# Decay products by two scans on 96 partitions, and another order of loads and first units, in a chunked attention with a gated feed-forward network

## The chip, the cores and the metric

One core of one Trainium2 chip. The time is device time of one execution in microseconds (us), the median of several runs. Each run also has a profile's span, which is about 2 us shorter than its time. Ratios of two kernels are the mean time of the one's fast runs over the mean time of the other's fast runs of the same rounds on the same chip, so they are not quite the ratio of the medians quoted; the interval behind a ratio is its 95% interval. A run is called slow when it is over 1.5% above the fastest run of the same kernel. "Granted clock" is the TensorE clock that the throttle allowed, as a share of full speed; row PEclk of a page gives it in tenths.

## The reference

A linear attention with decay (4 batches, 8 heads, 768 tokens, state 16, head size 32), whose output, put together as 3072 tokens of 256, goes through a gated network with 1536 hidden columns.

```python
log_a = np.log(np.clip(a, 1e-06, 1.0))
for c in range(nc):                         # chunks of the sequence
    cum = np.cumsum(la, axis=-1)
    L = np.exp(cum[:, :, :, None] - cum[:, :, None, :]) * causal
    M = np.einsum('bhin,bhjn->bhij', Cc, Bc) * L
    y_intra = np.einsum('bhij,bhjd->bhid', M, xc)
    y_inter = np.einsum('bhin,bhnd->bhid', Cc, state) * np.exp(cum)[:, :, :, None]
    y[:, :, sl] = y_intra + y_inter
    state = decay_full * state + sum_j(Bx)
# then: ((y2 @ w_a) * (y2 @ w_b)) @ w_out
```

## The kernel before

The sequence is cut into six blocks of 128 tokens. Two batches of one block are a pair, so there are twelve pairs; pair 0 is the first two batches' block 0. For each pair the kernel loads B, C and x (`bn`, `cn`, `xn`), scales B and C with factors of the running product of `a`, transposes them, forms scores, masks them and multiplies by x: this last is the value product. The result feeds units (pair, part), each 8 matmuls with `Wa` and `Wb`. Units are what TensorE is filled with while other engines prepare the next pair.

The head issues its transfers from three engines. SyncE's queue begins with `a`, then come the first halves of B, C and x; ScalarE's queue carries the second halves; GpSimd issues the weights.

```python
    nc.sync.dma_start(a_sb, a.rearrange("b h (k q) -> (b h) k q", q=Q))   # 32 rows
    load1(nc.scalar, 0, 0, 1)      # B of pair 0
    load1(nc.sync, 0, 0, 0)
    load1(nc.scalar, 0, 1, 1)      # C of pair 0
    load1(nc.sync, 0, 1, 0)
    ...
    nc.gpsimd.memset(sel, 1.0)     # masks, then the identity, then the weights
    ...
    load_w(0)                      # first third of Wa, Wb
    ...                            # causal mask
    load_w(1, (0,))                # second third, Wa only
```

The decay products are six scans on 32 partitions (row = batch and head), one for each block, spread over the head. Factors for block 0 come first; those of blocks 1 to 5 follow as 40 small matmuls between units (0,1) and (0,2). Then:

```python
    go((0, 4))                     # a unit between the masks of pair 1 and its value product
    pv(1)                          # value product of pair 1
    state(0)
    state(1)
    go((0, 5), (1, 0), (1, 1), (1, 2))
    transposes(2)
```

## Time and profile before

| | before |
|---|---|
| time, median of 4 (lowest to highest) | 130.28 us (129.74 to 130.97) |
| span of the profiled run | 128.0 us |
| TensorE busy | 93% |
| (0,0), first unit, begins | 10.82 us |
| transposes of pair 1 / of pair 2 begin | 14.52 / 24.86 us |
| first output product begins | 28.18 us |

The prediction below shows the lines that carry this. The profile lines of the head that matter later were not among them; here is the timeline of all engines of the kernel before (start, length, engine and line, operation; in brackets the idle time before and what ended it):

```profile
0.79 0.40 SPq L132 DMA_DIRECT2D a_sb<-in_a_dram  x1
...
2.28 0.94 POOL L188 DMA_DIRECT2D Wa<-in_moe_w_a_dram  x1
...
5.43 0.41 DVE L262 TENSOR_TENSOR cm<-cn,fC 128x256 f16<-128x256 f32 x1
...
7.03 1.25 PE L201 MATMUL tc<-warm 128*128 128x512 f16 x5
...
8.72 0.63 ACT L247 ACTIVATE x<-xn 128x512 f16<-128x512 f32 x1 [0.94 <-DMA xn<-in_x_dram]
```

The load of `a` costs SyncE 0.40 us of issuing, GpSimd issues the first weights at 2.28, C of pair 0 is used at 5.43 without a wait, and x of pair 0 is in at 8.72. Warm-up matmuls work on nothing and are there to keep TensorE busy.

### The profile page before, as it was taken

How to read it: one execution, taken by the hardware profiler on the slowest of the kernel's cores; microseconds unless marked ns; L12 is line 12 of the kernel's file. 1: busy time of each engine (PE TensorE's matmuls, PEld its weight loads, DVE VectorE, ACT ScalarE, POOL GpSimd, SP SyncE). 2: the span in 40 equal slices, each digit the busy share in tenths (PEclk: the TensorE clock that was granted, in tenths of full speed). 3: DMA queues.
4: the chain of work that ended last, by engine and by line, in shares of the span. 5: the costliest groups of instructions: out<-in, count | busy, mean ns of one | idle time of the engine just before them, and what ended most of it. 6: DMA issues, size and time to landing. Idle time of an engine off the chain costs nothing.

```text
span 128.0 us, 4399 instructions
## 1 busy us (share of the span) xinstructions
PE 118.6 (93%) x1761; PEld 97.1 (76%) x1761; DVE 89.6 (70%) x178; ACT 66.5 (52%) x129; POOL 62.0 (48%) x106
## 2 busy tenths in 40 slices
PE   6969979799999999999999999999999999999960
PEld 2425757688887888888888888888888888888840
DVE  4676769658695976967958959959759569364420
ACT  3344567594836545455556456465445464564410
POOL 7966830799982925907828447338339100000000
PEclk9999999999999999999999999999999999999999
DMA  3999999775435666566456555565565310211203
GB/s 66 158 215 164 211 199 216 117 136 111 105 67 88 156 90 111 120 110 142 91 96 146 104 87 131 111 111 123 101 133 116 73 42 0 46 41 23 51 8 82
DMA packets 51555, 13.76 MB, mean 107 GB/s; under 512 B 45328, under 2 KB 51504, under 8 KB 51536
## 3 DMA queue, kind: packets, MB, share of 16 engines
q1 hardware_dynamic: 46560, 10.72, 43.8%
q0 software_dynamic: 3184, 2.36, 12.5%
q10 hardware_dynamic: 1792, 0.41, 1.6%
q8 instruction: 13, 0.21, 0.7%
q14 instruction: 6, 0.05, 0.1%
HBM read 11.13 MB, written 3.15 MB: 111 GB/s over the span
## 4 chain that ended last, share of the span: by engine, by line
PE 77%; DMA 9%; SPq 7%; POOL 1%; issue 1%; ACTq 1%; DVE 0%; POOLq 0%
PE ops L493 25%; PE aps L476 22%; PE bps L476 21%; DMA cn<-in_C_dram 9%; SPq L123 7%; PE SC L380 3%; PE SC L336 3%; PE SC L397 2%; ACTq L123 1%; POOL bm L262 1%; PE SC L313 0%; POOL cm L262 0%; DVE osb L506 0%; POOLq L451 0%; POOLq L262 0%
## 5 line engine op out<-in xcount | busy, mean ns | idle before, releaser
L486 DVE TENSOR_TENSOR hk<-bps,asb 128x512 f16<-128x512 f32 x72 | 49.2, 687 | 20.8 <-ACT asb L485 18.9
L485 ACT COPY asb<-aps 128x512 f32<-128x512 f32 x72 | 42.1, 587 | 17.9 <-PE aps L476 16.4
L476 PE MATMUL bps<-X2T,Wb 128*128 128x256 f16 x288 | 43.2, 273 | 1.1 <-ACT G L611 1.1
L476 PE MATMUL aps<-X2T,Wa 128*128 128x256 f16 x288 | 43.5, 273 | 0.1
L493 PE MATMUL ops<-Wo,hk 128*128 128x256 f16 x288 | 35.3, 273 | 0.0
L476 PEld LDWEIGHTS <-Wb 128*128 128x128 f16 x288 | 28.1, 98 | 4.5 <-issue 0.6
L493 PEld LDWEIGHTS <-hk 128*128 128x128 f16 x288 | 27.4, 98 | 4.1
L476 PEld LDWEIGHTS <-Wa 128*128 128x128 f16 x288 | 26.8, 98 | 4.8 <-issue 0.3
L370 DVE TENSOR_TENSOR t<-SC,causal 128x512 f16<-128x512 f32 x45 | 29.4, 681 | 1.3 <-ACT tmp L367 1.0
L451 POOL TENSOR_TENSOR sbd<-U,maskbd 128x512 f16<-128x512 f32 x10 | 11.5, 1154 | 21.1 <-DVE U L447 21.0
L508 ACT ACTIVATE osb<-ops 128x256 f32<-128x256 f32 x23 | 8.8, 383 | 23.6 <-PE ops L493 22.9
L249 POOL TENSOR_SCALAR x<-xn 128x512 f16<-128x512 f32 x9 | 13.4, 1489 | 0.8 <-DMA xn<-in_x_dram 0.2
L408 ACT ACTIVATE X2T<-SC 128x512 f16<-128x512 f32 x11 | 6.6, 597 | 5.1 <-PE SC L380 5.1
L262 POOL TENSOR_TENSOR bc<-cn,fC 128x128 f16<-128x128 f32 x16 | 6.1, 402 | 5.6 <-DMA cn<-in_C_dram 3.4
L262 POOL TENSOR_TENSOR t<-bn,fB 128x256 f16<-128x256 f32 x12 | 7.7, 639 | 0.1
L262 POOL TENSOR_TENSOR bc<-bn,fB 128x128 f16<-128x128 f32 x16 | 6.1, 401 | 0.0
L380 PEld LDWEIGHTS <-x 64*32 64x32 f16 x384 | 3.2, 91 | 3.2 <-ACT x L247 1.6
L201 PE MATMUL SC<-warm 128*128 128x512 f16 (+1 forms) x14 | 4.4, 453 | 1.2 <-DVE warm L150 1.2
L427 DVE STREAM_TRANSPOSE dt<-SC 128x64 f32<-128x64 f32 x9 | 2.2, 249 | 4.1 <-ACT X2T L408 4.1
L262 POOL TENSOR_TENSOR cm<-cn,fC 128x128 f16<-128x128 f32 (+1 forms) x5 | 2.1, 445 | 5.9 <-DMA cn<-in_C_dram 5.9
L368 POOL TENSOR_TENSOR t<-tmp,causal 128x512 f16<-128x512 f32 x3 | 3.5, 1156 | 3.1 <-ACT tmp L367 3.1
L380 PE MATMUL SC<-t,x 64*32 64x144 f16 (+1 forms) x352 | 4.8, 224 | 0.0
(69 smaller groups left out, 66.8 us busy)
## 6 DMA issues: line engine op xcount, KB each, us to landing
xn<-in_x_dram SPq DMA_DIRECT2D x23, 128.0 KB, 3.2
out_dram<-osb SPq DMA_DIRECT2D x46, 64.0 KB, 2.1
bn<-in_B_dram SPq DMA_DIRECT2D x23, 64.0 KB, 2.7
cn<-in_C_dram SPq DMA_DIRECT2D x23, 64.0 KB, 3.3
Wa<-in_moe_w_a_dram POOLq DMA_DIRECT2D x3, 256.0 KB, 6.8
Wb<-in_moe_w_b_dram POOLq DMA_DIRECT2D x3, 256.0 KB, 6.6
Wo<-in_moe_w_out_dram POOLq DMA_DIRECT2D x1, 768.0 KB, 10.2
xn<-in_x_dram ACTq DMA_DIRECT2D x1, 128.0 KB, 5.4
```

The lines of the kernel that those rows point to most:

```text
L123: return eng.dma_start(pair_in[p][which][64 * bt : 64 * bt + 64].rearrange("i h r n -> i h (r n)"), src.rearrange("h (i r) n -> i h (r n)" ...
L249: eng.tensor_scalar(xo, xi, XS, None, ALU.mult)
L262: return eng.tensor_tensor(out=out, in0=i0, in1=i1, op=ALU.mult)
L370: nc.vector.tensor_tensor(out=o_, in0=i_, in1=c_, op=ALU.mult)
L380: nc.tensor.matmul(py[bt][32 * g : 32 * g + 32, u * (Q + N) : u * (Q + N) + w], s["X16"][k, h, r, :], s["T1"][k, h, r, 0:w], start=(first ...
L408: nc.scalar.activation(out=X2T[:, p].rearrange("p u t q -> p t u q"), in_=s["PY"][:, :, :, 0:Q], func=AF.Copy, scale=YS / XS,)
L451: nc.gpsimd.tensor_tensor(out=Sbd.rearrange("p t (h d) -> p t h d", h=H), in0=U32[:, p].unsqueeze(2).broadcast_to((128, 2, H, D)), in1=mas ...
L476: nc.tensor.matmul(ps[:, kk * 2 * Q : (kk + 1) * 2 * Q], W[:, f, k * 128 : (k + 1) * 128], X2T[:, p, f].rearrange("p t q -> p (t q)"), sta ...
L485: nc.scalar.copy(asb, a_ps)
L486: return lambda: nc.vector.tensor_tensor(out=s["hk"][:, 2 * k2 : 2 * k2 + 2, :].rearrange("p k q -> p (k q)"), in0=b_ps, in1=asb, op=ALU.mult)
L493: nc.tensor.matmul(o_ps[:, 0:d_model], hk[:, k, bt * Q : (bt + 1) * Q], Wo[:, k, :], start=(k == 0), stop=(k == NK - 1), skip_group_check= ...
L508: nc.scalar.activation(out=o_sb, in_=o_ps[:, 0:d_model], func=AF.Copy, scale=1.0 / (YS * YS))
```

## The change

The intent: make the running products of all blocks with two scans on 96 partitions (three groups of two blocks) in place of six on 32; do all factor products in the idle time of the head; let GpSimd compute the gates; and have the first units of pair 1 run ahead of those that need the last weights.

```diff
-    nc.sync.dma_start(a_sb, a.rearrange("b h (k q) -> (b h) k q", q=Q))
+    nc.sync.dma_start(
+        a_sb.rearrange("p t q -> p (t q)"), a.rearrange("b h (k c) -> k (b h) c", k=KP)
+    )
...
-    nc.gpsimd.memset(sel, 1.0)              # and its affine_select: gone
+    nc.gpsimd.memset(ident, 1.0)            # identity now first
...
-    load_w(1, (0,))
+    load_w(1)
...
-        for k in range(lo, hi):
-            nc.vector.tensor_tensor_scan(Pr[:, k], a_sb[:, k], zero, 1.0, ALU.mult, ALU.add)
+        nc.vector.tensor_tensor_scan(Pr[:, t], a_sb[:, t], zero, 1.0, ALU.mult, ALU.add)
...
-    warmup(2, SC[3])                        # behind the first factor product
-    warmup(1, SC[3], 128)
+    factors_mm(F, 0, 1, KP)
...
-    v = factors_mm(1, NBLK)                 # between (0,1) and (0,2)
...
-    load_w(1, (1,))
     load_w(2)
...
-    go((0, 4))
     pv(1)
+    turn(1)
+    go((1, 0))
...
-    go((0, 5), (1, 0), (1, 1), (1, 2))
+    go((1, 2), (1, 3))
     transposes(2)
-    go((1, 3))
-    h = unit(1, 4)
+    go((0, 4))
+    h = unit(0, 5)
```

The cut parts are the 96-row constants, the gate operations on GpSimd and the places of (1,4) and (1,5).

More of the change, by code (lines that the diff above doesn't have):

```diff
@@ L52 @@
     NG = NBLK - 1
+    KP = NBLK // 2
+    KR = KP * BH
     j = np.arange(128)
-    bh = np.arange(BH)
-    p32 = np.zeros((BH, 128 + nb * NG), np.float32)
-    p32[:, 0:128] = (bh[:, None] % H) == (j // N % 2 * (H // 2) + j // (2 * N))[None, :]
+    row = np.arange(KR)
+    p96 = np.zeros((KR, 128 + nb * KP), np.float32)
+    p96[:, 0:128] = (row[:, None] % H) == (j // N % 2 * (H // 2) + j // (2 * N))[None, :]
     for b in range(nb):
-        p32[b * H : (b + 1) * H, 128 + b * NG : 128 + (b + 1) * NG] = 1.0
-    p32_t = nc.inline_tensor(p32, "p32")
+        for k in range(KP):
+            p96[k * BH + b * H : k * BH + (b + 1) * H, 128 + b * KP + k] = 1.0
+    p96_t = nc.inline_tensor(p96, "p96")
     const = ctx.enter_context(tc.tile_pool(name="const", bufs=1))
-    c32 = const.tile([BH, p32.shape[1]], f32, name="c32")
+    c96 = const.tile([KR, p96.shape[1]], f32, name="c96")
     headm = const.tile([128, H], f32, name="headm")
@@ L68 @@
     causal = const.tile([128, 2, Q], f16, name="causal")
-    sel = const.tile([BH, 2, NBP, H], f32, name="sel")
-    indm = c32[:, 0:128]
-    selb = c32[:, 128 : 128 + nb * NG]
+    indm = c96[:, 0:128]
+    selb = c96[:, 128 : 128 + nb * KP]
     big = ctx.enter_context(tc.tile_pool(name="big", bufs=1))
-    a_sb = big.tile([BH, NBLK, Q], f32, name="a_sb")
-    zero = big.tile([BH, Q], f32, name="zero")
+    a_sb = big.tile([KR, 2, Q], f32, name="a_sb")
+    zero = big.tile([KR, Q], f32, name="zero")
     Wa = big.tile([128, 2, d_ff], f16, name="Wa")
@@ L83 @@
     warm = big.tile([128, 512], f16, name="warm")
-    Pr = big.tile([BH, NBLK, Q], f32, name="Pr")
-    rmid = big.tile([BH, NBLK], f32, name="rmid")
-    selr = big.tile([BH, NBLK, 2, NBP * H], f32, name="selr")
+    Pr = big.tile([KR, 2, Q], f32, name="Pr")
+    rmid = big.tile([KR, 2], f32, name="rmid")
+    selr = big.tile([KR, 2, KP, NBP, 2, H], f32, name="selr")
     fB = big.tile([128, NBLK, 2, NBP, H], f32, name="fB")
     fC = big.tile([128, NBLK, 2, NBP, H], f32, name="fC")
-    hr = big.tile([BH, NG], f32, name="hr")
-    hs = big.tile([BH, NG], f32, name="hs")
-    hsx = big.tile([BH, nb, NG], f32, name="hsx")
-    G = big.tile([128, nb, NG], f32, name="G")
+    nxt = big.tile([KR, 2], f32, name="nxt")
+    hr = big.tile([KR, 2], f32, name="hr")
+    hs = big.tile([KR, 2], f32, name="hs")
+    hsx = big.tile([KR, nb, KP, 2], f32, name="hsx")
+    G = big.tile([128, nb, NBLK], f32, name="G")
     bc = [big.tile([128, 6, H, N], f16, name=f"bc{i}") for i in range(2)]
@@ L140 @@
     load1(nc.scalar, 0, 2, 1)
-    nc.scalar.dma_start(c32, p32_t.ap())
+    nc.scalar.dma_start(c96, p96_t.ap())
     load1(nc.sync, 0, 2, 0)
@@ L153 @@
         nc.vector.memset(t_[:, 0:4].rearrange("p k h n -> p (k h n)").bitcast(u32), 0)
-    nc.gpsimd.memset(sel, 1.0)
+    nc.gpsimd.memset(ident, 1.0)
     nc.gpsimd.affine_select(
-        out=sel,
-        in_=sel,
-        compare_op=ALU.is_equal,
-        fill=0.0,
-        base=0,
-        pattern=[[-H, 2], [-2 * H, NBP], [-1, H]],
-        channel_multiplier=1,
+        out=ident, in_=ident, compare_op=ALU.is_equal, fill=0.0, base=0, pattern=[[-1, 128]], channel_multiplier=1
     )
@@ L177 @@
     )
-    nc.gpsimd.memset(ident, 1.0)
-    nc.gpsimd.affine_select(
-        out=ident, in_=ident, compare_op=ALU.is_equal, fill=0.0, base=0, pattern=[[-1, 128]], channel_multiplier=1
-    )
     KC = 4 * 128
@@ L203, in warmup, with scan, factors_mm @@
             )
-    def scan(lo, hi):
-        for k in range(lo, hi):
-            nc.vector.tensor_tensor_scan(Pr[:, k], a_sb[:, k], zero, 1.0, ALU.mult, ALU.add)
-    def sel_over_mid(lo, hi):
-        nc.vector.reciprocal(rmid[:, lo:hi], Pr[:, lo:hi, 63])
-        nc.vector.tensor_tensor(
-            out=selr[:, lo:hi].rearrange("p k t c -> p k (t c)"),
-            in0=sel.rearrange("p t b h -> p (t b h)").unsqueeze(1).broadcast_to((BH, hi - lo, 2 * NBP * H)),
-            in1=rmid[:, lo:hi].unsqueeze(2).broadcast_to((BH, hi - lo, 2 * NBP * H)),
-            op=ALU.mult,
-        )
-    def factors_mm(lo, hi):
-        fps = psf.tile([128, 512], f32, name="fps", tag="ff")
-        F = fps[:, 0 : (hi - lo) * 2 * NBP * H].rearrange("p (k r c) -> p k r c", k=hi - lo, r=2)
-        for k in range(lo, hi):
-            for r in range(2):
-                for bt in range(2):
-                    nc.tensor.matmul(
-                        F[64 * bt : 64 * bt + 64, k - lo, r],
-                        Pr[:, k].rearrange("p (i r) -> p r i", r=2)[:, r],
-                        selr[:, k, bt],
-                        start=True,
-                        stop=True,
-                        skip_group_check=True,
-                        tile_position=(0, 64 * bt),
-                    )
-        return F.rearrange("p k r c -> p (k r c)")
+    def scan(t):
+        nc.vector.tensor_tensor_scan(Pr[:, t], a_sb[:, t], zero, 1.0, ALU.mult, ALU.add)
+        nc.vector.reciprocal(rmid[:, t : t + 1], Pr[:, t, 63:64])
+        nc.vector.tensor_scalar(
+            selr[:, t].rearrange("p k b t h -> p (k b t h)"), ident[0:KR, 0:KR], rmid[:, t : t + 1], None, ALU.mult
+        )
+    def factors_mm(F, t, lo, hi):
+        for r in range(2):
+            for bt in range(2):
+                nc.tensor.matmul(
+                    F[64 * bt : 64 * bt + 64, lo:hi, t, r],
+                    Pr[:, t].rearrange("p (i r) -> p r i", r=2)[:, r],
+                    selr[:, t, lo:hi, :, bt],
+                    start=True,
+                    stop=True,
+                    skip_group_check=True,
+                    tile_position=(0, 64 * bt),
+                )
     def flat(f, lo, hi):
@@ L535 @@
     warmup(1, SC[3], 128)
-    scan(0, 1)
-    sel_over_mid(0, 1)
-    v = factors_mm(0, 1)
-    nc.vector.reciprocal(flat(fB, 0, 1), v)
-    nc.scalar.copy(flat(fC, 0, 1), v)
-    warmup(2, SC[3])
-    warmup(1, SC[3], 128)
+    scan(0)
+    fps = bank("fps")
+    F = fps[:, 0 : NBLK * 2 * NBP * H].rearrange("p (k t r b h) -> p k t r b h", k=KP, t=2, r=2, b=NBP)
+    factors_mm(F, 0, 0, 1)
+    scan(1)
+    nc.vector.reciprocal(flat(fB, 0, 1), F[:, 0, 0].rearrange("p r b h -> p (r b h)"))
+    nc.scalar.copy(flat(fC, 0, 1), F[:, 0, 0].rearrange("p r b h -> p (r b h)"))
+    factors_mm(F, 0, 1, KP)
     scale_bc(0, 0, nc.vector)
     n1 = scale_bc(0, 1, nc.vector)
-    scan(1, 2)
     tb, tcp = bank("tb"), bank("tc")
-    transposes(0, [tb, tcp], nc.vector.tensor_copy, lambda: warmup(2, SC[3], 128))
-    scan(2, 3)
+    transposes(0, [tb, tcp], nc.vector.tensor_copy, lambda: factors_mm(F, 1, 0, KP))
+    nc.scalar.copy(flat(fC, 1, NBLK), fps[:, 2 * NBP * H : NBLK * 2 * NBP * H])
     warmup(1, SC[3])
@@ L579 @@
     warmup(1, tcp, 128)
-    scan(3, NBLK)
     h = unit(0, 0)
     turn(0)
-    sel_over_mid(1, NBLK)
     h()
     go((0, 1))
-    v = factors_mm(1, NBLK)
-    nc.vector.tensor_tensor(out=hr, in0=Pr[:, 0:NG, Q - 1], in1=rmid[:, 0:NG], op=ALU.mult)
-    nc.vector.tensor_tensor(out=hs, in0=hr, in1=Pr[:, 1:NBLK, 63], op=ALU.mult)
-    nc.vector.tensor_tensor(
-        out=hsx,
-        in0=hs.unsqueeze(1).broadcast_to((BH, nb, NG)),
-        in1=selb.rearrange("p (b g) -> p b g", b=nb),
-        op=ALU.mult,
-    )
     transposes(1, None, nc.vector.tensor_copy)
-    nc.scalar.copy(flat(fC, 1, NBLK), v)
     h = unit(0, 2)
@@ L606 @@
     load(4)
-    gps = bank("gps")
-    nc.tensor.matmul(
-        gps[:, 0 : nb * NG], indm, hsx.rearrange("p b g -> p (b g)"), start=True, stop=True, skip_group_check=True
-    )
-    nc.scalar.copy(G.rearrange("p b g -> p (b g)"), gps[:, 0 : nb * NG])
     mask(product(1, 1))
     h()
+    nc.gpsimd.memset(nxt, 0.0)
+    nc.gpsimd.tensor_copy(nxt[:, 0:1], Pr[:, 1, 63:64])
+    for k in range(KP - 1):
+        nc.gpsimd.tensor_copy(nxt[k * BH : (k + 1) * BH, 1:2], Pr[(k + 1) * BH : (k + 2) * BH, 0, 63:64])
+    nc.gpsimd.tensor_tensor(out=hr, in0=Pr[:, :, Q - 1], in1=rmid, op=ALU.mult)
+    nc.gpsimd.tensor_tensor(out=hs, in0=hr, in1=nxt, op=ALU.mult)
+    nc.gpsimd.tensor_tensor(
+        out=hsx,
+        in0=hs.unsqueeze(1).unsqueeze(1).broadcast_to((KR, nb, KP, 2)),
+        in1=selb.rearrange("p (b k) -> p b k", b=nb).unsqueeze(3).broadcast_to((KR, nb, KP, 2)),
+        op=ALU.mult,
+    )
     scale_bc(2, 1, nc.gpsimd)
@@ L616 @@
     tail(2, nc.gpsimd)
-    go((0, 4))
     pv(1)
+    turn(1)
+    go((1, 0))
+    gps = bank("gps")
+    nc.tensor.matmul(
+        gps[:, 0 : nb * NBLK], indm, hsx.rearrange("p b k t -> p (b k t)"), start=True, stop=True, skip_group_check=True
+    )
+    nc.scalar.copy(G.rearrange("p b g -> p (b g)"), gps[:, 0 : nb * NBLK])
+    go((1, 1))
     state(0)
     state(1)
-    go((0, 5), (1, 0), (1, 1), (1, 2))
+    go((1, 2), (1, 3))
     transposes(2)
-    go((1, 3))
-    h = unit(1, 4)
+    go((0, 4))
+    h = unit(0, 5)
     scores(2)
@@ L628 @@
     scale_x(2, nc.scalar)
-    h2 = unit(1, 5)
+    h2 = unit(1, 4)
     mask(product(2, 1))
+    h()
     mask(product(2, 2))
-    h()
+    h2()
+    go((1, 5))
     out_half(0, 0)
-    h2()
     scale(3)
```

## The prediction

> **What bounds the kernel now.** I read four views: the busy table and the slices, the chain of waits, the timeline of TensorE alone, and the timeline of all engines up to 30 us.
>
> ```profile
> span 128.0 us, 4399 instructions
> PE 118.6 (93%) x1761; PEld 97.1 (76%) x1761; DVE 89.6 (70%) x178; ACT 66.5 (52%) x129; POOL 62.0 (48%) x106
> ...
> PE   6969979799999999999999999999999999999960
> ...
> DMA  3999999775435666566456555565565310211203
> ```
>
> From about 25 us on TensorE never rests, and the chain of waits is nothing but matmuls from there to the end: what is won or lost before 25 us reaches the end one for one, and nothing later can repair it. The same slices show the DMA engines full in the head. So the question is when TensorE reaches its gap-free part, and with how much work done. The timeline of TensorE (start, length, engine, line, operation; in brackets the idle time before and who ended it):
>
> ```profile
> 10.82 0.80 PE L476 MATMUL aps<-X2T,Wa 128*128 128x256 f16 x4
> ...
> 13.21 1.38 PE L225 MATMUL fps<-selr,Pr 32*64 32x16 f32 x40
> 14.52 0.29 PE L313 MATMUL SC<-ident,bm 128*128 128x128 f16 x2
> ...
> 16.17 0.43 PE L336 MATMUL SC<-ct,bt 32*64 32x128 f16 x32 [0.38 <-DVE ct L323]
> ...
> 17.86 0.60 PE L476 MATMUL aps<-X2T,Wa 128*128 128x256 f16 x4
> 19.52 0.60 PE L476 MATMUL bps<-X2T,Wb 128*128 128x256 f16 x4 [1.06 <-ACT G L611]
> 20.05 0.45 PE L380 MATMUL SC<-t,x 64*32 64x144 f16 x32
> 20.42 0.61 PE L476 MATMUL aps<-X2T,Wa 128*128 128x256 f16 x4
> ...
> 24.86 0.28 PE L313 MATMUL SC<-ident,bm 128*128 128x128 f16 x2 [0.77 <-POOL bm L262]
> ```
>
> The reader should see three losses: 40 records of factor products (13.21 to 14.52), 1.06 us of waiting in unit (0,4), 0.77 us before the transposes of pair 2. At 24.86 nine units are done: (0,0) to (0,5), (1,0) to (1,2). A unit is 8 matmuls of 0.109 us, 0.87 us. What stands behind the waits:
>
> ```profile
> 12.27 0.61 POOL L262 TENSOR_TENSOR cm<-cn,fC 128x256 f16<-128x256 f32 x1 [1.12 <-DMA cn<-in_C_dram]
> ...
> 18.77 0.63 ACT L247 ACTIVATE x<-xn 128x512 f16<-128x512 f32 x1 [0.96 <-DMA xn<-in_x_dram]
> 18.80 0.10 PEld L476 LDWEIGHTS <-Wb 128*128 128x128 f16 x1 [0.62 <-DMA Wb<-in_moe_w_b_dram]
> ...
> 23.32 0.76 POOL L262 TENSOR_TENSOR cm<-cn,fC 128x128 f16<-128x128 f32 x2 [4.76 <-DMA cn<-in_C_dram]
> ```
>
> The last weights arrive at 18.80, but x of pair 1 arrives at 18.77: the same moment. C of pair 1 arrives at 12.2, C of pair 2 at 23.3. All of them are transfers.
>
> [...]The old load of `a` has 32 rows on both sides; the new one has 96 on the chip and 3 x 32 in memory[...]. [...]the second x transfer of pair 1, whose issue ended at 10.3, landed only at 18.77 beside the weights. [...]The trace shows the rise (the first warm-up loads are 0.43 us apart; later 256-column matmuls 0.109 us), and no fall after an idle 1.13 us. [...]128 elements take 0.40 us, 2.1 ns each after 0.13 us fixed (the one-element reciprocal), against about 1.1 ns in the 128x256 product of 0.436 us. [...]96 rows cost what 32 do.
>
> **The change, part by part.**
> 1. Scans: six of 0.40 us become two. The second (with reciprocal and selector about 0.75 us, from 0.41 + 0.15 + 0.18) fits the 0.90 us in which VectorE waited for the first factor product. Three scans at 10.98 to 12.01 vanish; they held the transposes that free the bank of unit (0,1), so that starts about 0.27 us earlier.
> 2. [...]A 256-byte packet takes 18 ns, 1 KB on the weight queue 96 ns[...]. The first scan moves from 2.97 to about 4.2. The head then ends about 0.5 us later (u = 1 waits for the masks at about 10.4 instead of x), (0,0) starts near 11.3 and (0,1) ends near 13.3.
> 3. The 1.31 us of factor products leave. The transposes of pair 1 are then held by bm, ready on GpSimd at 13.55 because C lands at 12.2. They start near 13.6 instead of 14.51: 0.9 us gained, not 1.31.
> 4. The chain after them moves with it: scores 1.66 us later (14.51 to 16.17 before), 15.2; last VectorE mask 3.68 us after that (16.17 to 19.85 before), 18.9. But x of pair 1 lands at 18.77 and takes 0.63 us: 19.40. Moving the second Wb load from 8.96 to 5.9 closes a restart of the weight queue (around 11 us its first packets took 0.3 to 1.2 us in the packet records, and the window 10 to 12 us moved 149 GB/s against 212 before it), so landings may be up to 0.6 us earlier. I take the value product of pair 1 at 19.2. TensorE has finished (0,3) at about 16.5 and has nothing else: it stands still some 2.7 us, where before it did half of (0,4).
> 5. Unit (1,0) needs the evacuation of that product: 1.26 us after its start before (20.05 to 21.31), so 20.45. Before, (0,5) filled that gap; now nothing does. Four units (3.50) and the decay product (0.35, from 17.51 to 17.86) end at 24.3. Transposes of pair 2: 24.86 if C of pair 2 lands as before, 24.3 if 0.6 us earlier. I take 24.6.
> 6. But only eight units are done there. Before, 3.32 us from these transposes to the first output product (24.86 to 28.18). Now one unit more, 0.87. And in the built program the b half of (1,5) waits for the copy of (1,4), which ScalarE does after the mask copy and x of pair 2 (28.51 to 29.09 in the old timeline): about 0.45 us of stall. Sum 4.64: output product at 29.25 against 28.18, 1.07 us late.
>
> From there the programs agree: 129.99 + 1.07 = 131.06, about 131.1 us. GpSimd's seven small gate operations cost nothing; it waited 4.76 us there.
>
> **The rivals.** (a) The intended outcome: factor products gone (1.31) and the wait of 1.06 gone, 2.4 us faster, 127.6. For it: both are plain losses of TensorE. Against it: pair 1 waits for x, which lands with the last weights, and pair 2 for its C; the idle time moves. It would need x about 2 us and C 1 us earlier. (b) A wash, 129.5 to 130.3: landings 0.6 to 1 us earlier thanks to the continuous weight queue, and no bank stall. For it: the dip at 10 to 12 us is real. Against: the units behind. (c) The clock: 2.7 us of idle, and fewer warm-ups between 4 and 6 us; if it falls to half, up to 1.7 us more, 132 to 133.[...] (d) [...](0,1) ends after 13.55, and each further 0.1 us goes to the end.
>
> **Range and chances.** The sum gives +1.07. Landings 0.6 us earlier and no stall leave about +0.1; landings as before give +1.35; a clock drop or a slow `a` adds 1 to 1.5. That the change may have been tuned on the chip weighs a little for the lower side. So 131.1, range 129.5 to 132.6. Over 2% faster (below 127.4) needs rival (a): 0.04. Over 2% slower (above 132.6): 0.09. Within 2%: 0.87.
>
> **What would show it.** Right: landing of `a` near 3.3 us instead of 2.1; the first scan near 4.2; an idle TensorE of over 2 us before the value product of pair 1, ended by ScalarE's x or the masks; a gap of about 0.8 us before (1,0), ended by the evacuation; transposes of pair 2 between 24.1 and 24.9; a short stall in (1,5); the first output product near 29.3. Wrong: that product before 28.2, x of pair 1 in before 17.5, or matmuls of twice their length after the idle stretch. My weakest link is when the transfers land under the new order of the queues.

## The result, and the profile after

The changed kernel takes 135.97 us (135.11 to 136.04, 4 runs), the kernel before 130.28 in the same rounds: ratio 1.0419 (1.035 to 1.0487). It is 4% slower, outside the predicted range. The page of the changed kernel:

```profile
span 134.3 us, 4337 instructions
...
PE   6278972999899999999999999999999999999960
...
PEclk9999998569999999999999999999999999999999
```

A slice is 3.36 us here. Row PE has a 2 in the second slice and another in the seventh (20 to 23.5 us), and row PEclk reads 8, 5, 6 in slices 7 to 9: the granted clock fell to half there (0.50 in the window 24 to 26). In the kernel before, row PEclk is 9 in all 40 slices.

The same timeline of all engines in the head as above, now of the changed kernel:

```profile
0.80 0.95 SPq L136 DMA_DIRECT2D a_sb<-in_a_dram  x1
...
1.92 0.94 POOL L184 DMA_DIRECT2D Wa<-in_moe_w_a_dram  x1
...
5.82 0.42 DVE L203 TENSOR_TENSOR_SCAN Pr<-a_sb,zero 96x128 f32<-96x128 f32 x1 [3.67 <-DMA a_sb<-in_a_dram]
...
9.24 0.43 DVE L249 TENSOR_TENSOR cm<-cn,fC 128x256 f16<-128x256 f32 x1 [0.95 <-DMA cn<-in_C_dram]
...
11.16 1.74 PE L197 MATMUL tc<-warm 128*128 128x512 f16 x5
...
12.67 0.63 ACT L234 ACTIVATE x<-xn 128x512 f16<-128x512 f32 x1 [0.75 <-DMA xn<-in_x_dram]
```

The inputs of pair 0 are late: B by 2.79 (scaled at 7.86 instead of 5.07), C by 3.81, x by 3.95. For B that is the lateness of the first scan (2.85); for C and x it is more, and x does not depend on the scan at all: its line says that it waited for its transfer. (0,0), in the next view, begins at 14.76. TensorE is also slower in this head: the five warm-ups take 1.74 us instead of 1.25, and it stood still for 2.69 us, from 4.10 to 6.79. The first rise of the clock is recorded at 12.20 instead of 5.00; what row PEclk shows ahead of that record is not to be relied on, for it reads 9 while the first seven warm-ups take 2.85 us (ten of the same shape take 2.33 at full rate, as b_order_fill below shows). In this run the slower head cost (0,0) nothing, since x came last (the value product waited 0.44 us for it). TensorE further on:

```profile
14.76 0.80 PE L463 MATMUL aps<-X2T,Wa 128*128 128x256 f16 x4
...
21.61 0.24 PE L367 MATMUL SC<-t,x 64*32 64x144 f16 x4 [1.86 <-POOL nxt L586]
22.12 0.43 PE L367 MATMUL SC<-t,x 64*32 64x144 f16 x28 [0.26 <-DVE t L357]
23.25 1.01 PE L463 MATMUL aps<-X2T,Wa 128*128 128x256 f16 x4 [0.71 <-ACT X2T L395]
24.06 1.06 PE L463 MATMUL bps<-X2T,Wb 128*128 128x256 f16 x4
```

The wait of 1.86 us ahead of the value product is labelled with GpSimd's `nxt`, a small copy that it has nothing to do with; the masks of VectorE, two records from 20.79 to 22.07, are what it needs. Then come 0.26 and 0.71 us of waiting, and the matmuls of (1,0) take 1.01 and 1.06 us where one record took 0.60. The windows of the changed kernel (busy time of each engine, then granted clock, DMA share and GB/s) show the same:

```profile
22.00:24.00 2.00, 1.18 (x32) 0.90 (x32) 0.91 (x3) 0.60 (x1) 0.67 (x4) 0.61 1.42 189
24.00:26.00 2.00, 2.00 (x12) 1.53 (x11) 0.69 (x1) 0.77 (x2) 1.69 (x5) 0.50 1.31 213
```

Laid beside each other, the two profiled runs give this account:

| begins at | before | after | difference | step |
|---|---|---|---|---|
| (0,0) | 10.82 | 14.76 | +3.94 | +3.94: pair 0's inputs late |
| transposes of pair 1 | 14.52 | 16.71 | +2.19 | -1.75: factor products gone, no wait for C of pair 1 |
| transposes of pair 2 | 24.86 | 29.80 | +4.94 | +2.75: (1,0) to (1,3) take 6.55 us instead of some 3.8 |
| first output product | 28.18 | 34.49 | +6.31 | +1.37: one unit more left to do, and a stall in (1,5) |

In the third row the kernel before did one unit more between these two points; the standstill takes the place of that unit, so that the slower matmuls are the whole of the difference. Behind the first output product the programs run alike: spans 134.3 and 128.0 differ by 6.3. The two large terms are the head and the clock. Neither is the thing that the change was about, so the question for the experiments is which part of the diff each comes from.

### The profile page after: what moved, and what is told of

It is laid out like the page before. It is cut to its first block, busy times and chain, and to the rows that moved or that the text cites. A ratio compares the mean times of both kernels' runs of the same rounds, so it can differ in the third digit from the quotient of the medians.

```text
span 134.3 us, 4337 instructions
## 1 busy us (share of the span) xinstructions
PE 121.2 (90%) x1732; PEld 98.6 (73%) x1732; DVE 88.2 (66%) x171; ACT 66.6 (50%) x129; POOL 62.8 (47%) x111
## 4 chain that ended last, share of the span: by engine, by line
PE 80%; DMA 7%; ACT 4%; DVE 3%; SPq 2%; issue 1%; ACTq 0%
PE ops L480 24%; PE aps L463 24%; PE bps L463 23%; DMA xn<-in_x_dram 7%; PE SC L367 3%; PE SC L323 3%; PE SC L384 2%; DVE t L357 1%; DVE hk L473 1%; SPq L127 1%; ACT x L234 1%; ACT asb L472 1%; ACT bt L309 1%; SPq L136 1%; PE py L367 1%
## 5 line engine op out<-in xcount | busy, mean ns | idle before, releaser
L463 PE MATMUL aps<-X2T,Wa 128*128 128x256 f16 x288 | 45.1, 281 | 0.7 <-ACT X2T L395 0.7
L463 PE MATMUL bps<-X2T,Wb 128*128 128x256 f16 x288 | 44.6, 279 | 0.4 <-ACT asb L472 0.4
L463 PEld LDWEIGHTS <-Wb 128*128 128x128 f16 x288 | 28.8, 100 | 4.5 <-issue 0.5
L463 PEld LDWEIGHTS <-Wa 128*128 128x128 f16 x288 | 27.8, 101 | 5.8 <-issue 0.7
L213 PE MATMUL fps<-selr,Pr 96*64 96x16 f32 (+2 forms) x24 | 1.9, 296 | 3.4 <-DVE selr L205 2.7
L197 PE MATMUL SC<-warm 128*128 128x512 f16 (+1 forms) x9 | 3.6, 557 | 1.2 <-DVE warm L156 1.2
## 6 DMA issues: line engine op xcount, KB each, us to landing
xn<-in_x_dram SPq DMA_DIRECT2D x23, 128.0 KB, 3.1
xn<-in_x_dram ACTq DMA_DIRECT2D x1, 128.0 KB, 6.3
```

What stands on the lines that cost most here:

```text
L463: nc.tensor.matmul(ps[:, kk * 2 * Q : (kk + 1) * 2 * Q], W[:, f, k * 128 : (k + 1) * 128], X2T[:, p, f].rearrange("p t q -> p (t q)"), sta ...
```

## The experiments

In the expectations, theory A is that the load of `a` itself delays everything; B is that the standstill of TensorE makes the clock fall and that this is what costs; C is that the new order of units costs; D is that pair 0's inputs must get through before the weights begin; E is about the second Wb load. Numbers given as times in the run come from its profile.

### The load of `a`, the clock, the order: a16, a_fill, a16_fill, a16_old

`a16` cuts the load into three of 32 rows, so that each has 32 rows on both sides, as the load before had:

```diff
-    nc.sync.dma_start(a_sb.rearrange(...), a.rearrange("b h (k c) -> k (b h) c", k=KP))
+    for k in range(KP):
+        nc.sync.dma_start(a_sb[k * BH : (k + 1) * BH].rearrange(...), a.rearrange(...)[k])
```

> The changed kernel with its load of `a` cut into three loads of 32 rows each, so that each has 32 rows on both sides[...]; nothing else differs. Theory A[...]: first scan back from 5.8 to about 3.5 us, x of pair 0 lands near 9 instead of 12.6, unit (0,0) starts near 11 instead of 14.8, and the time falls by 2 to 4 us, to 132 to 134. If the clock also holds, 131 as forecast. Rival (the earlier second Wb load, not the load of `a`, made x of pair 0 late): scan early, but x still lands after 12 us, (0,0) still near 14, time still above 135.

Measured: 136.01 us against 129.88, ratio 1.0499 (1.0409 to 1.0588). The first scan came at 4.63 instead of 5.82, but C of pair 0 was used at 9.49, x at 12.07 and (0,0) began at 14.79: nothing won. Theory A falls in its simple form. The three loads together took SyncE 1.50 us to issue, and pair 0's B behind them was scaled at 7.83, as in the changed kernel (7.86).

`a_fill` leaves the load as in the changed kernel and puts matmuls on nothing into the standstill; `a16_fill` does both:

```diff
+    fill = bank("fill")
+    warmup(10, fill)
     pv(1)
+    warmup(3, fill)
     turn(1)
```

> The changed kernel with its slow load, plus 10 idle matmuls of 512 columns ahead of the value product of pair 1 and 3 after it, so that TensorE does not stand still there. Theory B (the standstill lets the clock fall to half, which costs the four units of pair 1 about 0.85 us each): granted clock 1.00 throughout, units (1,0) to (1,3) at 0.87 us each instead of 1.7, time down by 2 to 3 us, to 133 to 134. Rival (the clock falls for another reason, or the units would have waited for pair 2's inputs anyway): time within 1 us of 136.

> Both: three loads of 32 rows and the idle matmuls. If A and B are the whole of what the forecast mis-sized, this lands where the forecast did, 130.5 to 131.7, still slower than before by about 1 us, because of the order of the units (theory C: one unit fewer is done when pair 2's transposes start). Rival: with both mended the change is what was intended, below 128.5.

Measured: 134.37 us, ratio 1.0338 (1.027 to 1.0407), and 133.92 us, 1.0299 (1.0245 to 1.0353). In both, the clock was 1.00 behind the filler and a unit of pair 1 took 0.87 us. So the filler is worth 2.6 us between a16 and a16_fill (1.0499 to 1.0299), which is B. It was hoped that both together come near 131, and they did not, because the head had not moved: in a16_fill (0,0) began at 14.79. In the profiled run of a_fill it was at 16.50, with an unchanged head program. There C of pair 0 was used at 11.01 instead of 9.24, and the granted clock was 0.50 from 8.1 to 14.9 us. So between two executions of the same head (16.50 here, 14.76 in the changed kernel) its end differed by 1.74 us.

`a16_old` is a16 with the old order of the units, (0,4) ahead of the value product:

```diff
+    go((0, 4))
     pv(1)
     turn(1)
-    go((1, 0))
+    go((0, 5))
     ...                       # and (1,3), (1,4), (1,5) in their old places
```

> Three loads of 32 rows, the two scans and the early factor products kept, but the units in the order of the kernel before ((0,4) ahead of the value product of pair 1, (0,5) after it). Theory C: (0,4) and (0,5) fill the stalls, the clock holds without idle matmuls, and the removed factor products show at last: 128 to 129.5. Rival (pair 2's inputs set the end of the head whatever is ahead of them): 129.7 to 130.5, no gain over before.

Measured: 132.19 us, 1.0157 (1.01 to 1.0214); clock 1.00, transposes of pair 2 at 27.02 instead of 28.48. The order with the clock is worth 4.4 us here (1.0499 to 1.0157), more than the filler alone. What remains is 1.6%. I read it as the head, which was still late ((0,0) at 15.73); this run does not show it alone.

### What makes pair 0 late: a16_wlate, b_wearly, b_a3, b_wlate

Two things in the diff stand ahead of pair 0's inputs: a longer issue of `a` on their queue, and weights that start sooner because GpSimd has one mask fewer to make (issue at 1.92 instead of 2.28). Each was put into the kernel before by itself, and the weights were moved in both directions.

```diff
 b_wearly:  -    nc.gpsimd.memset(ident, 1.0) ... (identity ahead of the weights)
                 load_w(0)
            +    nc.gpsimd.memset(ident, 1.0) ... (identity behind them)
 b_a3:      -    nc.sync.dma_start(a_sb, ...)
            +    for k in range(0, NBLK, 2):
            +        nc.sync.dma_start(a_sb[:, k : k + 2], ...[:, k : k + 2])
 b_wlate:   -    load_w(0)
                 ...             # causal mask
            +    load_w(0)
                 load_w(1, (0,))
 a16_wlate: as b_wlate, in a16
```

> The kernel before, with nothing changed but the first two weight loads issued ahead of the identity instead of behind it, 0.5 us earlier, as the change does by the way. Theory D: x of pair 0 lands later than 8.7, (0,0) starts after 11, 0.5 to 2 us slower than before. Rival: no difference, within 0.4 us.

> The kernel before, with its load of `a` cut into three loads of 256 columns: 96 packets of 1 KB instead of 32 of 3 KB, and two more issues (0.5 us each) ahead of pair 0's inputs on the same queue. The first scan needs the first only. Theory D: scan on time near 3.0, but B, C and x of pair 0 pushed behind the weights, (0,0) near 13, time up by 2 to 3 us. Rival A (only the scan's own lateness counts): (0,0) within 0.5 us of 10.8, time as before.

> The kernel with three loads of `a` (a16), with the first pair of weight loads issued about 1.2 us later on GpSimd, behind the building of the causal mask. Theory D (once the weights flow, from about 3.7 us, the inputs of pair 0 that have not passed are held up until 6 us and later; the longer load of `a` and the earlier weights both push them there): C of pair 0 is used by 7.5 instead of 9.9, unit (0,0) starts near 12 instead of 14.8, time down by 2 us or more from 136.0. Rival A (the load of `a` alone holds them): (0,0) stays later than 14 and the time within 1 us of 136.

> The kernel before with the first two weight loads issued behind the causal mask, about 1.2 us later (near 3.5 instead of 2.28): the other direction of the dose of b_wearly. Theory D: the second x transfer of pair 0, the only one caught in before, passes too: x of pair 0 sooner than 8.7, (0,0) up to 1 us sooner, but the weights and everything behind them later by about 1 us, so time within 1% of before (129 to 131). If only lateness of weights counted: 131 or more.

| run | time (us) | ratio to before | C of pair 0 used | x of pair 0 | (0,0) |
|---|---|---|---|---|---|
| b_wearly | 134.84 | 1.0409 (1.0314 to 1.0504) | 7.08 | 9.87 | 12.33 |
| b_a3 | 135.23 | 1.0477 (1.0379 to 1.0575) | 9.97 | 12.55 | 15.74 |
| a16_wlate | 134.84 | 1.0388 (1.029 to 1.0485) | 8.95 | 12.09 | 14.19 |
| b_wlate | 130.75 | 1.0049 (1.0001 to 1.0098) | 5.62 | 7.81 | 10.07 |

Either delay alone, in an otherwise unchanged kernel before, costs about as much time as the whole change. But each dose is larger than the change's own. b_wearly issues the weights 0.51 us earlier (1.77), the change 0.36. The three issues of b_a3 take 1.50 us together, and pair 0's first input issue on SyncE comes 1.08 us later (2.33 instead of 1.25), in the change 0.55 later (1.80). The times also hold stretches at half clock: from 17.3 to 24.2 us in b_wearly, from 8.5 to 15.3, inside the head, in b_a3. At (0,0) b_a3 loses 4.92 us and b_wearly only 1.51; its total of 5 us is far more than the 0.5 to 2 expected. One line of b_a3, then two of b_wearly, from timelines of all engines:

```profile
8.05 0.42 DVE L263 TENSOR_TENSOR bm<-bn,fB 128x256 f16<-128x256 f32 x1 [3.02 <-DMA bn<-in_B_dram]
```

```profile
12.48 3.06 DVE L208 TENSOR_TENSOR_SCAN Pr<-a_sb,zero 32x128 f32<-32x128 f32 x3
...
15.71 0.60 PE L476 MATMUL aps<-X2T,Wa 128*128 128x256 f16 x4 [2.15 <-DVE dt L430]
```

In b_a3 the scan is on time (2.57) and the scaling of B waits 3.02 us for B; the inputs are what is late. In b_wearly C is 1.65 us late, and then three scans keep unit (0,1) waiting 2.15 us more. The scans stand at the same place in the kernel before, where all three took 1.03 us. Here one of them took 2.41 us (12.82 to 15.23), the others about 0.40. GpSimd's three products of pair 1 (13.14 to 14.95) fell into it, while before they began only after the scans; that they stretched it is not shown by a run. The changed kernel has no scans there, so this part of b_wearly's loss is not in it.

The mechanism is in the DMA queues (packets, MB, share of the 16 engines' time; q1 and q10 carry inputs from the two issuing engines, q0 the weights). Up to 4.5 us, in the kernel before:

```profile
q1 hardware_dynamic: 991, 0.22, 23.6%
q10 hardware_dynamic: 1165, 0.16, 21.3%
```

and in the changed kernel:

```profile
q10 hardware_dynamic: 957, 0.12, 16.7%
q1 hardware_dynamic: 451, 0.11, 12.8%
q0 software_dynamic: 20, 0.02, 4.2%
```

Before, 2124 input packets are through by 4.5 us (2156 less the 32 of `a`); in the changed kernel 1347 (1428 less 61 of `a` and 20 of the weights; `a` has 35 more to come), and the weights have begun. The same count is 1601 in b_wearly, 1447 in b_a3 and 2283 in b_wlate. (They are the packets under 512 B; those of `a` and of the weights are larger.) What happens after that moment is seen in the two microseconds from 4.5 to 6.5, in the kernel before, where the weights flow, and in b_wlate, where they do not yet:

```profile
q0 software_dynamic: 235, 0.23, 81.1%
q10 hardware_dynamic: 406, 0.10, 23.8%
q1 hardware_dynamic: 153, 0.02, 7.1%
```

```profile
q1 hardware_dynamic: 1067, 0.20, 58.3%
q0 software_dynamic: 33, 0.03, 25.7%
q10 hardware_dynamic: 387, 0.10, 23.4%
```

Beside the weights 559 input packets pass in 2 us, without them 1454. So with the weights the inputs passed at 1/2.6 of the rate (280 packets per us instead of 727), and some 780 missing packets at 280 per us are about 2.8 us (an estimate from these counts; the 280 are of all inputs, also those of pair 1, so it can be more). This is theory D, and b_wearly, b_a3 and b_wlate fit it in direction. It is not proportional: 1.3 us later weights (b_wlate, issued at 3.62) bring (0,0) forward by 0.75 but no time, since the weights and C of pair 1 are later too (transposes of pair 1 at 14.76, after a wait of 0.87), and its clock fell there (0.94 in the window 15.0 to 15.5, 0.50 after).

a16_wlate missed its expectation: C at 8.95 and not by 7.5, (0,0) at 14.19 and not near 12 (0.6 us won of 2.8), x at 12.09 where a16 had 12.07. By 4.5 us, with no weight packet through yet, 1530 input packets had passed (1099 in a16, 2124 before), so what held these back was not the weights. SyncE's three issues still stood ahead of pair 0. That counts against a story of the weights alone.

### The order and the clock apart: b_order, b_order_fill

`b_order` is the kernel before with only the order of the units of the change. `b_order_fill` adds the filler.

```diff
-    go((0, 4))
+    fill = bank("fill")              # b_order_fill only
+    warmup(10, fill)                 # b_order_fill only
     pv(1)
+    warmup(3, fill)                  # b_order_fill only
+    turn(1)
+    go((1, 0), (1, 1))
     state(0)
     state(1)
-    go((0, 5), (1, 0), (1, 1), (1, 2))
+    go((1, 2), (1, 3))
     transposes(2)
```

> The kernel before, with nothing changed but the order of units: the value product of pair 1 and (1,0) to (1,3) ahead of (0,4) and (0,5), as in the change. Theory C, by the forecast's sum: a stall of 1 to 2 us ahead of the value product, one unit fewer by the transposes of pair 2, 1.0 to 1.5 us slower if the clock holds; with Theory B 3 us or more slower, with (1,0) to (1,3) at 1.7 us each. Rival (the order was the useful part of the change): faster than before by 0.5 us or more.

> The kernel before with the new order of units alone (measured: 133.07 us, its four units after the stall at half clock), plus the same 10 fillers of 512 columns before the value product of pair 1 and 3 before its evacuation. If the clock was the larger part of the loss by the order (theory B): full clock in the units of batch 1 (0.87 us each instead of 1.5), transposes of pair 2 at about 24.6 instead of 26.80, output product near 29.3, time near 131 (one unit fewer and a stall in (1,5) remain, about 1 us). If order costs the time in another way: still 133.

Measured: 133.07 us, 1.0251 (1.0155 to 1.0348), and 130.69 us, 1.0064 (1.0002 to 1.0126). TensorE's timeline of b_order, and then of b_order_fill, around unit (1,0):

```profile
18.94 0.24 PE L380 MATMUL SC<-t,x 64*32 64x144 f16 x4 [1.45 <-DVE t L370]
19.44 0.67 PE L380 MATMUL SC<-t,x 64*32 64x144 f16 x28 [0.26 <-DVE t L370]
20.80 1.01 PE L476 MATMUL aps<-X2T,Wa 128*128 128x256 f16 x4 [0.69 <-ACT X2T L408]
```

```profile
17.32 2.33 PE L201 MATMUL fill<-warm 128*128 128x512 f16 x10
...
20.76 0.60 PE L476 MATMUL aps<-X2T,Wa 128*128 128x256 f16 x4
...
28.54 0.60 PE L476 MATMUL bps<-X2T,Wb 128*128 128x256 f16 x4 [0.38 <-ACT asb L485]
```

With fillers the record of `aps` takes 0.60 us, without 1.01. (1,0) begins at the same time in both. So the order itself costs 0.64%, 0.83 us, and the clock 2.4 us more. The last line is the stall in (1,5) that the prediction had: 0.38 us.

### Both delays of the head mended: rw, rwo, and a flaw of mine

The mended version puts the rows of the scans in the order batch, head, third. Then `a` is 96 rows of 1 KB one after the other in memory, and one load has 96 rows on both sides. GpSimd's old small mask is put back, so that the weights are issued at 2.29. The shift by one row that the gates need is done by a small transfer on SyncE's queue.

```diff
-    nc.sync.dma_start(a_sb..., a.rearrange("b h (k c) -> k (b h) c", k=KP))
+    nc.sync.dma_start(a_sb..., a.rearrange("b h (k c) -> (b h k) c", k=KP))
+    nc.gpsimd.memset(sel, 1.0) ...          # only for its time
+    nc.sync.dma_start(nx1[0 : KR - 1], Pr[1:KR, 0, 63:64])   # ahead of load(4)
```

> The changed kernel with both delays of the head taken away: the decay factors in rows (batch, head, third), so that the load of `a` is 96 rows of 1 KB contiguous in one transfer[...] with the issue time of before, and GpSimd's old small mask put back ahead of the first weight issue (2.28 us instead of 1.92). Theory D (pair 0's inputs must pass before the weights begin): x of pair 0 at about 8.7 again and unit (0,0) at 10.8 or a little sooner instead of 14.76. The order of units and the clock fall stay (theories B, C): a stall of over 2 us before the value product of pair 1, half clock after it, time near 132 to 133. If D is false, (0,0) stays near 14 and the time near 135.

> As rw, with the old order of units as well, (0,4) ahead of the value product of pair 1: all losses found removed, the two scans and the factor products in the head kept. D, B and C together: (0,0) near 10.8, no half clock, transposes of pair 2 at 24 to 24.6, time 128.5 to 130, up to 1% below before. If the scans on 96 rows themselves cost something: above 130.5.

Measured: 141.69 us, 1.0852 (1.0777 to 1.0926), and 141.57 us, 1.0716 (1.0631 to 1.0802), the slowest of all. The inputs of pair 0 were as theory D said: in rwo the first scan at 2.84, C of pair 0 used at 5.94 and x at 8.97. By 4.5 us 2126 input packets had passed, as before (2124). (0,0) began at 12.46, behind matmuls at half rate in the head (its five warm-ups took 2.31 us, before 1.25). The rest was my own mistake, seen in rwo's timeline of all engines:

```profile
26.38 0.89 SPq L586 DMA_DIRECT2D nx<-Pr  x1
...
28.65 0.18 POOL L592 COPY nxt<-nx 96x1 f32<-96x1 f32 x1 [9.60 <-DMA nx<-Pr]
```

The small transfer stands in SyncE's queue behind loads that were themselves late; it was issued at 26.38, and GpSimd waited 9.60 us for it, with TensorE behind GpSimd. These two runs say nothing on the time of the mended version. They showed one thing more: C of pair 1 was used at 13.51 in rwo and 14.82 in rw (slow), where it is 12.27 before. That raised theory E, the earlier second Wb load.

### The second Wb load, and the mended version: b_w1, rwo2, rwo2_w1, rw2

```diff
 b_w1:     (before)  -    load_w(1, (0,))
                     +    load_w(1)
                     -    load_w(1, (1,))            # behind the masks
 rwo2:     (rwo)     -    nc.sync.dma_start(nx1...)
                     +    nc.scalar.dma_start(nx1...)   # empty queue
                     +    warmup(2, SC[3])           # behind the first factor product
                     second Wb load as in the kernel before
 rwo2_w1:  rwo2 with the second Wb load early
 rw2:      rwo2 with the new order of units
```

> The kernel before with only the second Wb load moved up to 5.9 us, next to the second Wa load, as in the change. If the earlier Wb load is what holds pair 1's inputs (new theory E): C of pair 1 lands 1 to 2.5 us later than 12.2, transposes of pair 1 later by as much, time 131 to 133. If it closes a gap of the weight queue for free (step 4 of the prediction): inputs of pair 1 as before or sooner, time within 1% of 130.

> rwo with its helper transfer moved to ScalarE's empty queue, two warm-up matmuls put back behind the first factor product, and the second Wb load behind the masks as in the kernel before. Only the scans on 96 partitions, the factor products in the head and the small gate operations on GpSimd remain of the change. Expected: (0,0) at 10.8 to 11.2, C of pair 1 near 12.2 to 12.5, transposes of pair 1 near 13.6, no wait for the decay product, time 128.5 to 130. If the parts kept are worth nothing: 130.0; if they cost: above 130.8.

> rwo2 with the second Wb load early, as in the change. Theory E: C of pair 1 lands 1 to 2.5 us later than in rwo2 and the time is 1 to 3 us above rwo2. Without E: equal within 0.5 us.

> rwo2 with the new order of units. Theories B and C: a stall of over 2 us ahead of the value product of pair 1, the clock at half for some 6 us, time about 3 us above rwo2 (3.2 in the kernel before).

| run | time (us) | ratio to before | C of pair 1 used | transposes of pair 2 |
|---|---|---|---|---|
| b_w1 | 130.23 | 0.9977 (0.9936 to 1.0018) | 13.27 | 25.21 |
| rwo2 | 129.64 | 0.9937 (0.9893 to 0.9981) | 13.02 | 25.98 (profile slow) |
| rwo2_w1 | 131.65 | 1.0073 (1.003 to 1.0117) | 13.98 | 25.14 |
| rw2 | 134.03 | 1.0184 (1.0131 to 1.0237) | 13.51 | 28.49 (profile slow) |

In the kernel before, the earlier Wb load makes C of pair 1 a microsecond later and C of pair 2 four earlier (19.40 instead of 23.32), and the time is the same. Between rwo2 and rwo2_w1 it costs 1.4%; but the profiled run of rwo2_w1 has its transposes of pair 2 sooner than that of rwo2, so where this 1.4% sits is not shown. I leave theory E open for the mended version; for the kernel before it is refuted.

The order costs 2.5% again between rwo2 and rw2 (0.9937 to 1.0184), as in the kernel before (2.51%). The profiled run of rw2 is slow, so its details are not used.

### A version that beats both: rwo4 and rwo3

In rwo2 and rwo2_w1 the small transfer costs ScalarE 1.3 to 1.5 us of issuing, and the scores of pair 1 wait behind it. The timeline of all engines of rwo2_w1 (that of rwo2 is slow):

```profile
14.21 1.49 ACTq L575 DMA_DIRECT2D nx<-Pr  x1
...
17.45 0.43 PE L329 MATMUL SC<-ct,bt 32*64 32x128 f16 x32 [0.95 <-DVE ct L316]
```

`rwo4` replaces the transfer by a matmul of 95 rows and one column in the head, and does the gate operations in GpSimd's wait for C of pair 1. `rwo3` has seven warm-up matmuls instead of five ahead of pair 0's value product.

```diff
-    nc.scalar.dma_start(nx1[0 : KR - 1], Pr[1:KR, 0, 63:64])
+    nc.scalar.mul(nx1, Pr[:, 0, 63:64], Pr[:, 0, 63:64])
+    nc.tensor.matmul(fps[0 : KR - 1, 256:257], selr[:, 0]...[:, 1:KR], nx1, ...)
-    warmup(5, tcp)                            # rwo3 only
+    warmup(7, tcp)                            # rwo3 only
```

> rwo2 without its helper transfer: the shift by one row as one small matmul in the head, the gate operations on GpSimd in its wait for C of pair 1. If the transfer's 1.33 us on ScalarE counted: scores of pair 1 at 16.0 to 16.6 instead of 18.25, time 128.3 to 129.5 beside a kernel before at 130. If x of pair 1 limits anyway, as in the prediction: as rwo2, 129.6.

> rwo4 with seven warm-up matmuls instead of five ahead of pair 0's value product. If the clock in (0,0) to (0,1) matters: fewer slow runs and up to 1 us less than rwo4; if not, equal.

Measured: rwo4 129.26 us, 0.9913 (0.9863 to 0.9962); rwo3 129.02 us, 0.9867 (0.9806 to 0.9927), and two of its six runs slow (131.81 and 130.22), so the fewer slow runs hoped for did not come. These two are not in the ratio; with them its mean is 129.42 against 130.09, 0.995. All six runs of rwo4 were fast. The scores of pair 1 came at 16.73 in rwo4, just outside the expected 16.0 to 16.6. By their fast runs both beat the kernel before by about 1%; their intervals overlap, so the two extra warm-ups are not shown to help. TensorE's side of rwo3, timeline of all engines:

```profile
12.42 0.80 PE L469 MATMUL aps<-X2T,Wa 128*128 128x256 f16 x4
...
15.07 0.29 PE L306 MATMUL SC<-ident,bm 128*128 128x128 f16 x2 [0.55 <-POOL bm L255]
...
24.41 0.28 PE L306 MATMUL SC<-ident,bm 128*128 128x128 f16 x2
```

(0,0) begins 1.60 us later than before (12.42). The inputs are not the reason, for C of pair 0 is used at 5.95 (before 5.43); the factor products of the other blocks now stand in the head, where TensorE works at half rate for longer (first rise recorded at 10.01, before at 5.00; the seven warm-ups take 2.26 us). But the transposes of pair 1 only 0.55 later, since no factor products stand between them; at the transposes of pair 2 it is 0.45 us ahead. So the parts that gave the change its name are worth about 1%.

## Why the prediction was wrong

It said 131.1 us and a range of 129.5 to 132.6; the kernel took 135.97. By its own steps:

- Step 1, scans: right. Two scans of 0.41 to 0.42 us do the work of six; one on 32 rows took 0.41 (the first of the kernel before).
- **Step 2 failed, and is the main error.** It put the delay of the first scan at 1.2 us, an estimate of mine that no trace showed, and concluded "(0,0) starts near 11.3". The first half was too small, for the scan came at 5.82 and not 4.2. A packet of the load took 46 ns (the median of the packet records), but the packets began at 2.72 instead of 1.81 and took 2.33 us together in place of 0.63, with at most 5 under way at once against 14 before. But the worse fault is the mechanism. It took the load of `a` as the only thing delayed. The runs show that the head is set by pair 0's B, C and x, that their first halves stand behind `a` on the same queue and all of them pass beside the weights, and that the issue of `a` went from 0.40 to 0.95 us while the weights began 0.36 us sooner. The second delay was read nowhere in the prediction, although the diff shows the mask leaving GpSimd. b_a3 (+4.92 us at (0,0)) and b_wearly (+1.51) show that each kind of delay, in a larger dose than the change's, makes the head late; with both taken away (rwo), C and x of pair 0 are back at 5.94 and 8.97. How the change's loss divides between the two is not shown. The term was +0.5 us; it measured +3.94 in the profiled run.
- Step 3: the factor products are gone, and the transposes of pair 1 gain 1.75 us relative to (0,0), more than the 0.9 of the step, because in a head that late C of pair 1 is nearly in (a wait of 0.16).
- Step 4: the standstill came as told, with 1.86 and 0.26 us recorded as waits, ended by the masks. Its guess that moving the second Wb load brings landings forward was right in b_w1 for x of pair 1 (used at 17.66 instead of 18.77) and for C of pair 2, and wrong for C of pair 1; it moved no time in b_w1.
- Step 5: the gap ahead of (1,0) came (0.71 us, ended by the evacuation). "Four units (3.50)" failed by the clock: with the decay product they took 6.55 us.
- Step 6 was right: one unit fewer, and the stall in (1,5) is 0.36 us. With the clock held, the order alone measured 0.83 us against the +1.07 of the prediction.
- Rival (c), the clock, was named with "up to 1.7 us more" and set aside; no trace had shown what makes the clock fall. b_order and b_order_fill show the fall is real, and costs 2.4 us: the second step that failed, in size and in its being set aside.
- Rival (d), a load of `a` that costs over 2 us, came true by its condition (the first scan was 2.85 us later), but not by its mechanism: a16 brought the scan forward to 4.63, and (0,0) stayed at 14.79.
- Two slips did no harm. By the prediction's own steps the low end of the sum is +0.3 and not +0.1 (24.3 + 3.32 + 0.87 = 28.49, against 28.18). And the 0.13 us taken as the fixed part of a VectorE operation belongs to the five-element reciprocal; the one-element form takes 0.15.

The timed runs add up in the same way. From the kernel before to rwo2 the time falls by 0.6% (0.8 us of 130), from rwo2 to rw2 it rises by 2.5% (3.2 us, order and clock), and from rw2 to the changed kernel by a further 2.4% (3.1 us: the form of the load, the earlier weights, the second Wb load and two missing warm-ups, less what rw2's small transfer costs). The ratios are of different rounds, and by their intervals each term is good to about 0.7 to 0.9%. How the last 2.4% divides among its five parts is not shown. Nor is the part of TensorE's half rate in the late heads: in b_wearly, b_a3 and a16 the value product of pair 0 followed its masks and warm-ups without waiting for x, so there it may count.

## What to carry to other kernels

In a head like this one, where beside the weights 559 input packets passed in 2 us and without them 1454, the thing to count is how many input packets are through when the weights begin. Here 0.55 us of issue time on one queue and one small operation less on the engine that issues the weights made the first unit 3.94 us late. When a reorder leaves TensorE standing, count the slower matmuls after the gap and not only the gap (2.4 us of clock here, against 0.83 us for the order itself), and test it by putting fillers into it. And keep a helper transfer off a queue whose loads run late: a one-column matmul did in 0.48 us what had waited 9.6.

## What the runs show of the clock, the queues and the load of `a`

- In b_order TensorE stood from 17.49 to 18.94, and the clock fell at about 19.1 (granted mean 0.64 in the window 19.0 to 19.5, 0.50 after), with TensorE busy up to 1.65 us before. The length of one idle stretch does not decide it alone: the clock fell in b_wlate after 0.87 us and not in the kernel before after 1.06. What does decide it, no run shows.
- Small inputs beside a large load: input packets were 1454 in 2 us in b_wlate, where the weights had hardly begun (33 packets), and 559 in the kernel before, where 235 weight packets took 81% of the engines' time. How the queues share the engines, no run shows.
- The form of the load of `a`: one load from 3 x 32 rows in memory into 96 on the chip had its 96 KB used 5.0 us after its issue began, against 2.2 us before; as 96 rows in one piece 2.1 us. The records show at most 5 packets of the first under way at once, against 14 before. Why, the times do not settle, for in a16, with 32 rows in each load, the first scan still came at 4.63. The issue time went from 0.40 to 0.95 us for the same 96 KB.
